# Four buffers instead of three for x and the exponentials, and two moved steps for batches 3 and 4, in a cross-attention and ReGLU kernel

## The chip, the cores and the metric

The kernel runs on one core of a Trainium2 chip. The metric is the device time of one execution in microseconds (us), from the first to the last work of the core; lower is better. Times of runs are medians of several executions. A profile shows one execution, and the times inside it are us from the start of its span.

## The reference

There are 8 batches and 8 heads. Per batch and head, x is 512 rows by 64 and the state is 32 rows by 64. Both attend to each other, and the joined rows go through a gated feed-forward block:

```python
scale = 1.0 / np.sqrt(D)                                  # B, H, S, Ns, D = 8, 8, 512, 32, 64
a  = softmax(scale * x @ state.T)                         # x reads the state
xread = a @ state
a2 = softmax(scale * state @ x.T)                         # the state reads x
sread = a2 @ x
h = concatenate([xread, sread], axis=2)                   # 544 rows a batch, 512 wide after joining heads
gate, val = relu(h @ w_gate), h @ w_val                   # 512 -> 1536
out = (gate * val) @ w_out                                # 1536 -> 512
```

Inputs and output are float32. The kernel computes the matrix products in bfloat16.

## The kernel before, in words

**The work.** The exponentials `e_sn` of the scores serve both softmaxes, since a row sum and a column sum of the same numbers are taken. For a batch b, x comes in as float32 (`xf`), is converted to bfloat16 (`xb`), and is transposed (`xT`). `att_sc` multiplies xT with the transposed state into `sc_ps`, `att_exp` takes the exponential on ScalarE, and `att_norm` sums and divides on VectorE into `a_sn`, which is transposed into `ANS`. The state times the gate and value weights is formed first (`U`), so that the feed-forward input of the 512 x rows is ANS times U. `sr_half` forms the other direction, the state rows, from `e_sn` and `xb`: it is the last reader of both. Eight batches, b = 0 to 7, each have two halves of heads (0 and 1), so `sr_half(0, 1)` is the second half of batch 0.

**Slices.** Each batch is cut in 12 slices jf = 0 to 11 of 128 columns of the 1536. A slice "b.jf" issues, in this order: four matmuls `gv` (L286), `relu` on ScalarE (L311), `mult` on VectorE (L315), and four matmuls of the output product of an earlier slice (`out_piece`, L328). Every third output piece ends a row block: ScalarE copies it (L336) and SyncE's queue (SP) stores it (L337). Behind that, a slice issues the further steps that the table `at(b, jf, step, ...)` names for it, in the order of the calls. The loop is

```python
    for g in range(first, NF * (B + 1)):
        b, jf = divmod(g, NF)
        gv(b, jf) if b < B else gvs(jf)
        relu(b, jf)
        mult(b, jf)
        if g >= lag:
            out_piece(*divmod(g - lag, NF))
        for f in units.get(g, ()):
            f()
```

**What sets the order.** Each engine runs its instructions in the order in which the kernel issues them; no scheduler reorders them. The order in time between engines comes from semaphores that follow the data and from the reuse of buffers: a tile that takes a buffer over waits until the last reader of the tile before it is done. x of batches 1 and 2 is loaded with conversion; x of batch 3 is loaded as float32 by GpSimd (POOL) at the end of its list of loads (`x_dma(3, (nc.gpsimd,))`, L100), and the later ones by SP.

**The steps of the change.** `x_next(b)` is three instructions: two conversions of half a batch on POOL (L147) and one transposing transfer on SP's queue (L154) from `xb` to `xT`. `x_dma(b, (nc.sync,))` is one transfer of 1024 KB on SP's queue (L100) into `xf`, which has two buffers. Slice 2.2 issues `sr_half(0, 0)` and `sr_half(2, 0)`; slice 2.3 issues `sr_half(0, 1)` and then `att_half(3, 0)`, which begins with the score matmuls of batch 3 (L182) that read `xT`; slice 2.4 issues `sr_half(1, 0)` and `sr_half(2, 1)`, slice 2.5 `sr_half(1, 1)` and `att_half(3, 1)`. `xb` and `e_sn` had three buffers each, held by batches 0, 1 and 2 when batch 3 begins; the first of them to be read out is that of batch 0, by `sr_half(0, 1)`.

Of the kernel before, what the change touches and what calls it, by code (L numbers as in the profile page):

```python
# [9 lines left out]
BF16 = mybir.dt.bfloat16  # L10
# [6 lines left out]
def kernel(  # L17
# [9 lines left out]
    nc = tc.nc  # L27

    B, H, S, D = x.shape
    Ns = state.shape[2]  # L30
# [3 lines left out]
    NC = S // 128  # L34
# [3 lines left out]
    def pool(name, bufs, space=None):  # L38
        if space is None:
            return ctx.enter_context(tc.tile_pool(name=name, bufs=bufs))  # L40
        return ctx.enter_context(tc.tile_pool(name=name, bufs=bufs, space=space))
# [4 lines left out]
    att = pool("att", 2)  # L46
# [9 lines left out]
    NK = 2  # L56
    HK = H // NK
# [18 lines left out]
    xf, xb, xT, e_sn, a_sn, ANS, U, hsb, sr_sb = {}, {}, {}, {}, {}, {}, {}, {}, {}  # L76
    copy = {"act": nc.scalar.copy, "dve": nc.vector.tensor_copy, "pool": nc.gpsimd.tensor_copy}

    def bank(name, o=None):

        if o is None:
            return ps_r.tile([128, 512], FP32, name=name, tag="r")
        return ps_o.tile([128, 512], FP32, name=name, tag=f"o{o}")
# [16 lines left out]
            eng.dma_start(out=xf[b][:, i * n:(i + 1) * n], in_=src)  # L100

    def xb_alloc(b):
        xb[b] = att.tile([128, NC * H * D], BF16, name="xb", tag="xb", bufs=3)

    cast_on_load = set()

    def x_dma_cast(b):

        cast_on_load.add(b)
        xb_alloc(b)  # L110
        nc.gpsimd.dma_start(out=xb[b].rearrange("p (h c d) -> p h c d", h=H, c=NC),
                            in_=x[b].rearrange("h (p c) d -> p h c d", c=NC))
        xb[b] = xb[b].rearrange("p (h c d) -> p c h d", h=H, c=NC)
# [28 lines left out]
    def x_conv(b, half, eng):  # L142
        if half == 0:
            xb_alloc(b)
            xb[b] = xb[b].rearrange("p (c h d) -> p c h d", c=NC, h=H)
        hs = slice(HK * half, HK * half + HK)
        copy[eng](out=xb[b][:, :, hs].rearrange("p c h d -> p h c d"), in_=xf[b][:, hs])  # L147
# [25 lines left out]

    def att_sc(b, kc):
        if kc == 0:
            e_sn[b] = att.tile([128, NK, NC, HK * Ns], BF16, name="e_sn", tag="e_sn", bufs=3)
            a_sn[b] = att.tile([128, NK, NC, HK * Ns], BF16, name="a_sn", tag="a_sn")
        t = held["sc", b, kc] = bank("sc_ps")
        ps = t.rearrange("p (c j m) -> p c j m", c=NC, j=2)
        for c in range(NC):  # L180
            for jj in range(2):
                nc.tensor.matmul(ps[:, c, jj], xT[b][:, c, 2 * kc + jj], stT[:, b, 2 * kc + jj],  # L182
                                 start=True, stop=True)
# [218 lines left out]
    def spin(n):  # L402
        for i in range(n):
# [3 lines left out]

    steps = {"spin": spin, "stc": state_conv, "stT": state_T, "sto": state_out, "xc": x_conv, "xT": x_T, "xo": x_out,
             "sc": att_sc, "ex": att_exp, "nm": att_norm, "aT": att_T, "ao": att_out, "aD": att_aT_dma,
             "c": c_unit, "co": c_out, "ga": lambda b, jf: gv(b, jf, (0,)), "gb": lambda b, jf: gv(b, jf, (1,)),  # L410
             "re": relu, "mu": mult, "xn": x_next}
# [23 lines left out]
    def at(b, jf, f, *args):  # L435
        units.setdefault(NF * b + jf, []).append(lambda: f(*args))
# [21 lines left out]
    def att_up(b, kc):  # L458
        att_sc(b, kc)
        att_exp(b, kc)  # L460
        att_norm(b, kc)
# [23 lines left out]
    at(1, 10, att_pe, 2, 1)  # L485
    at(1, 11, u_block, 2, 512)
    at(2, 1, u_block, 2, 1024)
    at(2, 1, x_next, 3)
    at(2, 1, x_dma, 4, (nc.sync,))
    at(2, 2, sr_half, 0, 0)  # L490
    at(2, 3, sr_half, 0, 1)
    at(2, 4, sr_half, 1, 0)
# [19 lines left out]
    for g in range(first, NF * (B + 1)):  # L512
        b, jf = divmod(g, NF)
# [43 lines left out]
```

## Time and profile before

| | |
|---|---|
| median of 3 runs (lowest to highest) | 246.54 us (246.44 to 246.57) |
| the profiled execution: its own time / its span | 245.76 us / 244.0 us |
| busy: TensorE matmul (PE) / VectorE (DVE) / ScalarE (ACT) / GpSimd (POOL) | 226.0 / 145.1 / 123.5 / 27.9 us |
| share of PE in the chain of work that ended last | 83% |
| data moved | 25.72 MB, 105 GB/s in the mean |

How to read it: the page cuts the span in 40 slices of 6.1 us (not the kernel's slices). A digit is the busy share of an engine in tenths, and the row PEclk is the clock that TensorE was granted, in tenths of full speed. In the timeline a row has the start, the duration, the engine, the line and the operation, the tile written and the tiles read, and in square brackets how long the engine was idle before it and what ended that. "SPq" is the queue of SP; its rows are issues of transfers, not the transfers' own time. A matmul of 512 columns has a modelled duration of about 0.38 us, but the next one starts about 0.22 us later, so that the distance between starts is what it costs.

### The profile page before, as it was taken

Reading aid. Unit: us, or ns where it says so; the run is one execution under the profiler, and the core shown is the slowest. Engines: PE = TensorE matmul, PEld = TensorE weight load, DVE = VectorE, ACT = ScalarE, POOL = GpSimd, SP = SyncE. Lnnn points to the kernel's source line nnn. Section 1 sums busy time; section 2 is a strip of 40 time slices with the busy share of each in tenths; the row PEclk is TensorE's granted clock in tenths of the full one; section 3 lists DMA queues with packets and bytes.
Section 4 is the critical chain, followed back from the end, with each engine's and each line's share of the span. In section 5 each row is a group of like instructions: output and inputs, shape, how many; then the busy total and the mean of one; then the engine's idle time right before and its main releaser. Section 6 shows DMA issues by size and latency. Waiting matters only on the chain.

```text
span 244.0 us, 4511 instructions
## 1 busy us (share of the span) xinstructions
PE 226.0 (93%) x1759; PEld 110.6 (45%) x1788; DVE 145.1 (59%) x273; ACT 123.5 (51%) x238; POOL 27.9 (11%) x37
## 2 busy tenths in 40 slices
PE   6698999999089999999999999999999999999994
PEld 2453345345045345534553455345434544666543
DVE  1869785867149666776677667776777634222200
ACT  3768877654013663556355635563556344324221
POOL 8755010000303003000300030000000000000000
PEclk9999999999859999999999999999999999999999
DMA  6999994110471393139313921351141111111142
GB/s 203 183 196 198 223 217 167 46 43 0 79 225 43 80 226 121 46 83 213 142 45 81 259 93 44 84 134 42 46 87 43 46 44 44 46 43 43 64 111 86
DMA packets 36981, 25.72 MB, mean 105 GB/s; under 512 B 17280, under 2 KB 32384, under 8 KB 36960
## 3 DMA queue, kind: packets, MB, share of 16 engines
q1 hardware_dynamic: 25712, 17.31, 25.9%
q0 software_dynamic: 10368, 7.21, 18.5%
q10 hardware_dynamic: 880, 0.92, 1.3%
q8 instruction: 14, 0.23, 0.4%
q14 instruction: 7, 0.06, 0.1%
HBM read 18.35 MB, written 8.91 MB: 112 GB/s over the span
## 4 chain that ended last, share of the span: by engine, by line
PE 83%; DVE 5%; DMA 4%; ACT 2%; issue 2%; POOL 1%; SPq 0%; DVEq 0%; ACTq 0%
PE o_ps L328 35%; PE gv_ps L286 33%; PE gv_ps L304 4%; PE up L261 4%; PE sr_ps L222 3%; DMA xT<-xb 2%; DMA xf<-in_x_dram 2%; PE sc_ps L182 1%; DVE cs L192 1%; DVE a_sn L195 1%; DVE h_sb L315 1%; DMA out_dram<-o_sb 1%; POOL xb L147 1%; PE upc L261 1%; ACT e_sn L186 1%
## 5 line engine op out<-in xcount | busy, mean ns | idle before, releaser
L286 PE MATMUL gv_ps<-ans,U 128*128 128x512 bf16 x359 | 95.9, 382 | 1.5
L328 PE MATMUL o_ps<-wo_sb,h_sb 128*128 128x512 bf16 x370 | 95.8, 382 | 0.3
L311 ACT ACTIVATE g_sb<-gv_ps 128x512 bf16<-128x512 f32 (+1 forms) x108 | 62.5, 579 | 52.2 <-PE gv_ps L286 40.1
L315 DVE TENSOR_TENSOR h_sb<-gv_ps,g_sb 128x512 bf16<-128x512 f32 x96 | 65.5, 690 | 32.4 <-ACT g_sb L311 29.5
L328 PEld LDWEIGHTS <-h_sb 128*128 128x128 bf16 x372 | 36.6, 98 | 42.0 <-issue 1.1
L286 PEld LDWEIGHTS <-U 128*128 128x128 bf16 x384 | 33.7, 98 | 41.9 <-issue 9.6
L336 ACT COPY o_sb<-o_ps 128x512 f32<-128x512 f32 x31 | 18.1, 585 | 22.6 <-PE o_ps L328 22.6
L271 DVE CAST U<-up 128x512 bf16<-128x512 f32 x36 | 23.2, 686 | 6.8 <-PE up L261 6.8
L271 ACT CAST U<-up 128x512 bf16<-128x512 f32 x36 | 19.4, 592 | 11.1 <-PE up L261 11.1
L147 POOL CAST xb<-xf 128x1024 bf16<-128x1024 f32 x10 | 10.1, 1040 | 103.5 <-DMA xf<-in_x_dram 45.9
L192 DVE TENSOR_REDUCE cs<-e_sn 128x16 f32<-128x512 bf16 x16 | 11.0, 685 | 15.3 <-ACT e_sn L186 15.3
L186 ACT ACTIVATE e_sn<-sc_ps 128x512 bf16<-128x512 f32 x16 | 9.6, 600 | 13.0 <-PE sc_ps L182 13.0
L315 DVE TENSOR_TENSOR hs_sb<-gv_ps,g_sb 128x256 bf16<-128x256 f32 x12 | 5.1, 425 | 15.3 <-PE gv_ps L304 10.5
L182 PE MATMUL sc_ps<-stT,xT 128*128 128x64 bf16 x128 | 6.7, 196 | 7.0 <-DMA xT<-xb 6.6
L233 DVE TENSOR_SCALAR sr_sb<-sr_ps,rr 64x128 bf16<-64x128 f32 x32 | 11.2, 350 | 0.8
L195 DVE TENSOR_TENSOR a_sn<-e_sn,rc 128x512 bf16<-128x512 bf16 x16 | 11.1, 692 | 0.6
L222 PE MATMUL sr_ps<-xb,e_sn 128*128 128x256 bf16 x64 | 10.8, 275 | 0.0
L182 PEld LDWEIGHTS <-xT 128*128 128x128 bf16 x128 | 5.7, 100 | 10.4 <-DMA xT<-xb 6.8
L281 ACT CAST U<-upc 128x512 bf16<-128x512 f32 x18 | 9.9, 592 | 0.5 <-PE upc L261 0.5
L261 PEld LDWEIGHTS <-stT 64*32 64x32 bf16 x480 | 4.6, 89 | 11.7 <-issue 11.4
L224 PE MATMUL sr_ps<-ones,e_sn 128*128 128x1 bf16 x64 | 9.2, 166 | 0.0
L261 PE MATMUL up<-wv_sb,stT 64*32 64x512 bf16 x144 | 7.6, 376 | 0.1
(59 smaller groups left out, 138.0 us busy)
## 6 DMA issues: line engine op xcount, KB each, us to landing
out_dram<-o_sb SPq DMA_DIRECT2D x31, 256.0 KB, 2.3
xf<-in_x_dram SPq DMA_DIRECT2D x4, 1024.0 KB, 7.1
wg_sb<-in_moe_w_gate_dram POOLq DMA_DIRECT2D x6, 256.0 KB, 10.3
wv_sb<-in_moe_w_val_dram POOLq DMA_DIRECT2D x6, 256.0 KB, 10.5
wo_sb<-in_moe_w_out_dram POOLq DMA_DIRECT2D x2, 768.0 KB, 15.9
xb<-in_x_dram POOLq DMA_DIRECT2D x2, 512.0 KB, 9.7
xf<-in_x_dram POOLq DMA_DIRECT2D x1, 1024.0 KB, 19.0
xf<-in_x_dram ACTq DMA_DIRECT2D x2, 256.0 KB, 4.3
```

Source lines behind the costliest of these rows:

```text
L147: copy[eng](out=xb[b][:, :, hs].rearrange("p c h d -> p h c d"), in_=xf[b][:, hs])
L182: nc.tensor.matmul(ps[:, c, jj], xT[b][:, c, 2 * kc + jj], stT[:, b, 2 * kc + jj], start=True, stop=True)
L192: nc.vector.reduce_sum(out=cs, in_=e_v, axis=AX.X)
L195: nc.vector.tensor_tensor(out=a_sn[b][:, kc].rearrange("p c (h n) -> p (c h) n", n=Ns), in0=e_v, in1=rc.to_broadcast([128, NC * HK, Ns]), ...
L222: nc.tensor.matmul(ps[:, 0:256], e_sn[b][:, kc, c], xb[b][:, c, HK * kc:HK * kc + HK], start=(c == 0), stop=(c == NC - 1), skip_group_chec ...
L261: nc.tensor.matmul(dst[kc][q:q + 32], stT[r:r + 64, b, j, 32 * sl:32 * sl + 32], wsb[r:r + 64, j, lo:lo + n], start=True, stop=True)
L271: copy[eng](out=U[b][:, w, kc, lo:lo + 512], in_=held["u", b, w, lo][kc])
L286: nc.tensor.matmul(ps[w], U[b][:, w, kc, f0:f0 + 128], ANS[b][:, kc].rearrange("p c t -> p (c t)"), start=(kc == 0), stop=(kc == NK - 1))
L311: nc.scalar.activation(out=g_sb[:, 0:n], in_=ps[0][:, 0:n], func=AF.Relu)
L315: nc.vector.tensor_tensor(out=dst, in0=ps[1][:, 0:n], in1=held["g", b, jf][:, 0:n], op=ALU.mult)
L328: nc.tensor.matmul(o_ps[0], src[:, jf, tsub * 128:(tsub + 1) * 128], wo_sb[:, jf], start=(jf == 0), stop=(jf == NF - 1))
L336: nc.scalar.copy(out=o_sb, in_=o_ps[0])
```

## The change

`xb` and `e_sn` get a fourth buffer. `x_next(3)` is issued at the end of slice 2.0 instead of in slice 2.1, and `x_dma(4)` at the head of what slice 2.4 adds instead of in slice 2.1.

```diff
     def xb_alloc(b):
-        xb[b] = att.tile([128, NC * H * D], BF16, name="xb", tag="xb", bufs=3)
+        xb[b] = att.tile([128, NC * H * D], BF16, name="xb", tag="xb", bufs=4)
...
         if kc == 0:
-            e_sn[b] = att.tile([128, NK, NC, HK * Ns], BF16, name="e_sn", tag="e_sn", bufs=3)
+            e_sn[b] = att.tile([128, NK, NC, HK * Ns], BF16, name="e_sn", tag="e_sn", bufs=4)
...
     at(1, 11, u_block, 2, 512)
     at(2, 1, u_block, 2, 1024)
-    at(2, 1, x_next, 3)
-    at(2, 1, x_dma, 4, (nc.sync,))
+    at(2, 0, x_next, 3)
+    at(2, 4, x_dma, 4, (nc.sync,))
     at(2, 2, sr_half, 0, 0)
```

On POOL the instructions stay in the same order; what they wait for changes. The rows below are the end of POOL's list of loads and the first two pairs of conversions (batch 3, then batch 4); in the brackets are the semaphores waited for: DMASW1 is the load of `xf`, PE the last reader of the buffer that `xb` takes over.

```order
 L100 DMA xf<-in_x_dram 128x8x256 [waits DMASW1_49]
 L125 CAST st_b<-st_f 128x768 [waits DMASW6_49]
-L147 CAST xb<-xf 128x4x4x64 [waits DMASW1_49,DVE_49,PE_49]
+L147 CAST xb<-xf 128x4x4x64 [waits DMASW1_49]
 L147 CAST xb<-xf 128x4x4x64
-L147 CAST xb<-xf 128x4x4x64 [waits DMAHW0_49,DMASW5_49,PE_49]
+L147 CAST xb<-xf 128x4x4x64 [waits DMAHW1_49,DVE_49,PE_49]
 L147 CAST xb<-xf 128x4x4x64
```

The conversion of batch 3 no longer waits for TensorE or VectorE, only for its load; that of batch 4 now takes the buffer of batch 0, which the one of batch 3 took before.

On SP's queue one store changes its place. The rows run from the stores of the first two row blocks (L337), over the transpose of batch 3 (L154) and the load of batch 4 (L100), to the transpose of `a_sn` of batch 3 (L203).

```order
 L337 DMA out_dram<-o_sb 128x512 x2
 L154 DMA_TRANSPOSE xT<-xb 128x16x128
+L337 DMA out_dram<-o_sb 128x512
 L100 DMA xf<-in_x_dram 128x8x256
-L337 DMA out_dram<-o_sb 128x512 x2
+L337 DMA out_dram<-o_sb 128x512
 L203 DMA_TRANSPOSE ans<-a_sn 128x8x128
 L337 DMA out_dram<-o_sb 128x512
```

The store of the third row block (issued by slice 2.2) now stands ahead of the load of batch 4 and not behind it. The lists of PE, DVE and ACT are the same in both kernels.

## The prediction

> **What bounds the kernel now.** I read the head of the page first, then the 40 slices, then the list of waits, and last the timeline where those point.
>
> ```profile
> PE 226.0 (93%) x1759; PEld 110.6 (45%) x1788; DVE 145.1 (59%) x273; ACT 123.5 (51%) x238; POOL 27.9 (11%) x37
> ...
> PE   6698999999089999999999999999999999999994
> ...
> PEclk9999999999859999999999999999999999999999
> ```
>
> TensorE bounds the kernel as a whole, so only what stops or slows it counts. One digit of PE is 0: the eleventh slice, 61.0 to 67.1 us. There and in the slice behind it the granted clock is lower (8, then 5), and nowhere else. The list of waits between 61 and 80 us names the two long ones:
>
> ```profile
> POOL xb L147 <- PE sr_ps L224: 40.1, 2, 30.2
> ...
> PE sc_ps L182 <- DMA xT<-xb: 6.6, 1, 6.6
> ```
>
> The columns are the sum, the number of waits and the longest. The timeline of that place shows how they hang together:
>
> ```profile
> 60.69 0.27 PE L222 MATMUL sr_ps<-xb,e_sn 128*128 128x256 bf16 x1
> ...
> 61.44 2.02 POOL L147 CAST xb<-xf 128x1024 bf16<-128x1024 f32 x2 [30.16 <-PE sr_ps L224]
> ...
> 63.49 1.88 SPq L154 DMA_TRANSPOSE xT<-xb  x1
> 65.55 1.00 SPq L100 DMA_DIRECT2D xf<-in_x_dram  x1
> ...
> 67.97 0.61 PE L182 MATMUL sc_ps<-stT,xT 128*128 128x64 bf16 x8 [6.60 <-DMA xT<-xb]
> ```
>
> POOL stood for 30 us before the conversion of batch 3: the three buffers of xb belonged to batches 0, 1 and 2, and the first comes free when TensorE ends `sr_half(0, 1)` in slice 2.3. But the very next step of TensorE in that slice is the score product of batch 3, which needs conversion, transpose and landing. So the chain of conversion (2.0 us) and transpose (63.49 to 67.97) lies bare in TensorE's path.
>
> **What the pause costs.** Rows of the same steps at full clock, rows of the stretch behind the pause, and the clock there (the column 0.50 of the window):
>
> ```profile
> 56.16 1.04 PE L286 MATMUL gv_ps<-ans,U 128*128 128x512 bf16 x4
> 57.03 1.03 PE L328 MATMUL o_ps<-wo_sb,h_sb 128*128 128x512 bf16 x4
> 57.89 0.27 PE L222 MATMUL sr_ps<-xb,e_sn 128*128 128x256 bf16 x1
> 58.97 1.02 PE L286 MATMUL gv_ps<-ans,U 128*128 128x512 bf16 x3
> ...
> 73.16 0.38 PE L286 MATMUL gv_ps<-ans,U 128*128 128x512 bf16 x1
> ...
> 75.42 0.39 PE L182 MATMUL sc_ps<-stT,xT 128*128 128x64 bf16 x8
> 75.65 0.28 PE L239 MATMUL srT_ps<-id_91,sr_sb 128*128 128x128 bf16 x2
> ```
>
> ```profile
> 68.00:72.20 4.20, 4.20 (x19) 1.92 (x20) 2.32 (x4) 1.19 (x2) 0.00 (x0) 0.50 0.88 286
> ```
>
> Two `sr_half` take 58.97 - 57.89 = 1.08 us, one 0.54. The one that starts at 60.69 therefore leaves TensorE free at 61.23, and the score product starts at 67.97: 6.74 us of pause. Behind it stand scores, four gv, four output matmuls and two sr_half, up to the gv at 73.16: 5.19 us. At full clock these are 0.23 (75.42 to 75.65) + 0.87 (56.16 to 57.03) + 0.86 (57.03 to 57.89) + 1.08 = 3.04 us. The half clock costs 2.15 us more. Together TensorE would gain 8.89 us, if nothing else stopped it.
>
> **Part one: the fourth buffer of xb, and x_next(3) a slice earlier.** The conversion of batch 3 gets a buffer that nobody holds; its wait on TensorE is gone, and it waits only for its load.
>
> ```profile
> 22.40 0.89 POOL L100 DMA_DIRECT2D xf<-in_x_dram  x1 [0.52 <-DMA wg_sb<-in_moe_w_gate_dram]
> ...
> 44.88 7.67 SPq L337 DMA_DIRECT2D out_dram<-o_sb  x2
> ...
> 83.84 0.34 SPq L337 DMA_DIRECT2D out_dram<-o_sb  x1
> 84.28 1.91 SPq L154 DMA_TRANSPOSE xT<-xb  x1
> ```
>
> ```profile
> xf<-in_x_dram POOLq DMA_DIRECT2D x1, 1024.0 KB, 19.0
> ```
>
> ```profile
> DMA to landing us min/median/max: 4.4/4.4/5.6
> ```
>
> The load is issued at 22.4 and lands 19.0 us later, at 41.4 (42.3 if counted from the end of the issue). The two conversions then run to 43.4 or 44.3. On SP's queue the transpose stands behind the stores of two row blocks, the second of which ends its issue at 44.88 + 7.67 = 52.55. The transpose goes out there, right behind a store as at 83.84 and 84.28, and lands 4.4 to 5.6 us later (last fence: the five transposes into xT), at 57.0 to 58.2. TensorE asks at 61.23: 3.0 us to spare. The pause goes wholly, and with it its cause of the half clock. Behind the conversion on POOL stands only that of batch 4; behind the transpose on SP stand the store of slice 2.2 and the load of batch 4, and neither is held longer than now. Issuing x_next(3) in 2.0 instead of 2.1 passes nothing on either queue: 0.
>
> [...] The conversion of batch 3 moves from a quiet place to 41.4 to 44.3, where VectorE is busy with batch 2:
>
> ```profile
> 43.51 0.69 DVE L195 TENSOR_TENSOR a_sn<-e_sn,rc 128x512 bf16<-128x512 bf16 x1
> 44.12 0.42 DVE L171 COPY xT<-xT_ps 128x512 bf16<-128x512 bf16 x1
> ...
> 44.60 0.38 PE L182 MATMUL sc_ps<-stT,xT 128*128 128x64 bf16 x7 [0.33 <-DVE xT L171]
> ...
> 73.36 2.02 POOL L147 CAST xb<-xf 128x1024 bf16<-128x1024 f32 x2 [9.90 <-PE sr_ps L224]
> ...
> 74.73 0.69 DVE L315 TENSOR_TENSOR h_sb<-gv_ps,g_sb 128x512 bf16<-128x512 f32 x1
> ```
>
> A product under a conversion (74.73, inside 73.36 to 75.38) takes the usual 0.69 us, so the near row says 0. But that one reads PSUM and one SBUF tile; the division at 43.51 reads two SBUF tiles, and TensorE waits 0.33 us at 44.60 for the copy behind it, so what it loses TensorE loses. A bound: the division takes double, 0.69 us more; a gain is excluded, since the conversion gives VectorE nothing. I take 0, by the near row. [...]
>
> **Part two: the fourth buffer of e_sn.** The exponential of batch 3 follows the score product, and that follows `sr_half(0, 1)` on TensorE itself, so it finds batch 0's buffer free already: 0 us.
>
> **Part three: the load of batch 4 behind a store.** It stands behind the store whose copy is the first row here; the second row is the size and landing of such loads.
>
> ```profile
> 58.09 0.58 ACT L336 COPY o_sb<-o_ps 128x512 f32<-128x512 f32 x1 [0.47 <-PE o_ps L328]
> ```
>
> ```profile
> xf<-in_x_dram SPq DMA_DIRECT2D x4, 1024.0 KB, 7.1
> ```
>
> The store goes out at about 58.7, the load at about 59.1 (now 65.55), landing near 66.2. Its conversion then ends near 68.3 instead of 75.4 (73.36 + 2.02) and waits for its transpose, which stands behind the store at 83.84 less the gain. It has 7 us to spare. The load begins after xT of batch 3 has landed, so they share nothing: 0.
>
> **What is late next.** The pause also let VectorE catch up. Its rows from the reduction of batch 3 to the product of slice 2.6, and the first work of TensorE that waits for what follows (by the chain of waits):
>
> ```profile
> 61.65 0.71 DVE L233 TENSOR_SCALAR sr_sb<-sr_ps,rr 64x128 bf16<-64x128 f32 x2
> 69.24 0.69 DVE L192 TENSOR_REDUCE cs<-e_sn 128x16 f32<-128x512 bf16 x1 [6.89 <-ACT e_sn L186]
> ...
> 72.83 0.17 DVE L230 RECIPROCAL rr<-sr_ps 128x1 f32<-128x1 f32 x1 [1.16 <-PE sr_ps L224]
> ...
> 75.63 0.17 DVE L230 RECIPROCAL rr<-sr_ps 128x1 f32<-128x1 f32 x1 [0.21 <-PE sr_ps L224]
> ...
> 78.57 0.69 DVE L315 TENSOR_TENSOR h_sb<-gv_ps,g_sb 128x512 bf16<-128x512 f32 x1
> ...
> 80.68 0.23 DVE L245 COPY br<-srT_ps 64x128 bf16<-64x128 bf16 x1 [1.03 <-ACT br L245]
> ```
>
> ```profile
> 80.68 0.24 DVE br L245
> ...
> 80.96 0.40 PE up L261 x4
> ```
>
> From 69.24 to 78.57 VectorE needs 9.33 us with 1.37 us of idling, so 7.96 us without a gap. In the changed kernel the reduction can start at about 62.4: VectorE is done with `sr_norm` at 62.36, and the exponential's result comes no later behind the scores' start than now at half clock (69.24 - 67.97 = 1.27 us, so by 62.5). The product of slice 2.6 then starts at 70.36, 8.2 us earlier. Where nothing waits, a row starts before the last one ends (the row of 43.51 lasts 0.69 us, and the next starts 0.61 us after it); at the two joints where the idling vanishes that saves 0.08 us each: 8.2 to 8.4. I take 8.3. TensorE's `up` at 80.96 hangs on this chain, so from there the kernel is 8.3 us earlier and not 8.89; the difference is a longer wait there, by 0.6 us. VectorE idles 1.03 us in it, so its backlog ends at this place, and all that follows moves as a block.
>
> **Sum.** Against the profiled execution: 245.76 - 8.3 = 237.5 us. The median of the runs is 0.78 us above it: 246.54 - 8.3 = 238.2 us.
>
> **Rivals.**
> - *The division at 43.51 is held by the conversion.* For it: the two lie within 0.1 us or overlap, by when the load lands. Against: 74.73. Time 238.2 + 0.7 = 238.9.
> - *The clock falls all the same.* If the half clock is not the pause's doing, 2.15 us stay, VectorE has its time, and the gain is 6.74: 239.8. Against it: the clock is full in every other slice, where no such pause stands.
> - *The transpose lands late.* If it took twice the longest landing, 11.2 us from 52.55, TensorE would wait from 61.2 to 63.8, and the gain is 8.89 - 2.6 = 6.3: 240.2. Against: the five landings, of which 5.6 is the longest.
> - *It does nothing,* if the early conversion waits for something that I overlook: 246.5. Against: the wait on POOL named the last reader of the buffer, and that is gone.
> - *Slower: an unbroken TensorE is throttled.* From 61.2 us to the end of the span, 244.0 - 8.3 = 235.7, are 174.5 us. If they ran at a granted clock below 0.955, the 8.3 us would be lost (8.3 of 182.8); at 0.94 the time is 249.3. Against it, TensorE works 34.79 of the last 35 us before 240, after 130 us without a pause, at the full clock (the column 1.00):
>
> ```profile
> 205.00:240.00 35.00, 34.79 (x219) 21.53 (x221) 7.17 (x15) 10.54 (x24) 0.00 (x0) 1.00 0.20 69
> ```
>
> **How the numbers follow.** My forecast 0.85; the held division 0.05; the clock 0.03; the late transpose 0.03; nothing 0.02; slower 0.02. A difference under 0.2% (0.5 us) is about what a measurement cannot tell from none. Faster is the first four, 0.96; same 0.02; slower 0.02. The range begins at 237.0, somewhat under 246.54 - 8.89 = 237.7, since TensorE's wait at `up` could shorten where I let it grow, and ends at 239.4, half a us beyond the held division; the other cases, 0.10, are left out.
>
> **What would show it.** Right: no 0 in the PE row and no digit under 9 in PEclk; the conversion of batch 3 at 41 to 44 us behind its load, its transpose issued near 52.6, the load of batch 4 near 59; the score product at about 61.2 with no idle before it; the product of slice 2.6 near 70.3 and a longer wait at the `up` behind it. Wrong: a score product that still waits for xT, a low clock elsewhere, a division of over 0.8 us near 43.5, or a VectorE backlog that reaches beyond slice 2.8.

## The result, and the profile after

| | before | after |
|---|---|---|
| median of 4 runs (lowest to highest) | 246.49 us (245.76 to 246.57) | 238.22 us (237.82 to 240.09) |
| the profiled execution: its own time / its span | 245.76 / 244.0 us | 240.09 / 238.3 us |

The ratio of the times is 0.9687, with a 95% interval of 0.9635 to 0.9740. The forecast was 238.2 us. Two further executions of the changed kernel took 237.59 and 239.83 us. The two rows of the page of the changed kernel, TensorE's busy tenths and its clock in 40 slices of 6.0 us:

```profile
PE   6668999999999999999999999999999999999993
...
PEclk9979999999999999999999999999999999999999
```

The 0 in the PE row is gone, and so is the low clock in the slices where it stood. A 7 in PEclk is new, in the third slice, far ahead of the change; more of that below. The timeline of the changed kernel at the place of the old pause:

```profile
41.84 2.03 POOL L147 CAST xb<-xf 128x1024 bf16<-128x1024 f32 x2 [9.71 <-DMA xf<-in_x_dram]
...
55.41 1.99 SPq L154 DMA_TRANSPOSE xT<-xb  x1
61.43 0.34 SPq L337 DMA_DIRECT2D out_dram<-o_sb  x1
61.94 0.39 SPq L100 DMA_DIRECT2D xf<-in_x_dram  x1
...
63.42 0.27 PE L222 MATMUL sr_ps<-xb,e_sn 128*128 128x256 bf16 x1
...
63.96 0.39 PE L182 MATMUL sc_ps<-stT,xT 128*128 128x64 bf16 x8
```

The conversion now waits for its load alone and runs 20 us earlier; the transpose stands behind the second store; the score product follows `sr_half(0, 1)` after 63.96 - 63.42 = 0.54 us, the length of that step, with no idle time in brackets.

TensorE's rows lie 2.73 us later than forecast (63.42 against 60.69 for the same matmul), and the transpose, the store and the load with them within 0.15 us; only the conversion, which waits for its load alone, does not. The reason is the start of this one execution. These are the rows of the first transposes of x of batch 1 and the gv behind them, before and then after:

```profile
13.01 0.64 PE L165 MATMUL xT_ps<-id_91,xb 128*64 128x128 bf16 x16
13.58 1.90 PE L286 MATMUL gv_ps<-ans,U 128*128 128x512 bf16 x8
```

```profile
14.11 0.94 PE L165 MATMUL xT_ps<-id_91,xb 128*64 128x128 bf16 x16 [1.02 <-DMA xb<-in_x_dram]
14.98 3.22 PE L286 MATMUL gv_ps<-ans,U 128*128 128x512 bf16 x8
```

x of batch 1 landed a us late, and the eight gv took 3.22 us instead of 1.90; the clock was 0.50 from 14.28 to 17.68 us, and 1.00 in the same stretch of the kernel before. Both lie some 27 us ahead of the first step that the change moves, the conversion at 41.84. From there to the old pause the two executions run alike, so the gain is read from the shift: VectorE's product of slice 2.6, forecast at 70.2 to 70.4, against 78.57 before. Below it are the copies of the next step, `state_prep` (it transposes the state of batches 4 to 7), on VectorE and then on ScalarE, and TensorE's products `up`, the second half of which waits for them.

```profile
72.88 0.69 DVE L315 TENSOR_TENSOR h_sb<-gv_ps,g_sb 128x512 bf16<-128x512 f32 x1
73.49 0.47 DVE L139 COPY stT<-stT_ps 64x256 bf16<-64x256 bf16 x2
...
73.93 0.41 PE L261 MATMUL up<-wg_sb,stT 64*32 64x512 bf16 x8
...
74.05 0.63 ACT L139 COPY stT<-stT_ps 64x256 bf16<-64x256 bf16 x2 [3.12 <-DVE stT L139]
...
74.73 0.40 PE L261 MATMUL up<-wv_sb,stT 64*32 64x512 bf16 x4 [0.39 <-ACT stT L139]
75.28 0.40 PE L261 MATMUL up<-wv_sb,stT 64*32 64x512 bf16 x4
75.60 1.04 PE L286 MATMUL gv_ps<-ans,U 128*128 128x512 bf16 x3
```

It is 78.57 - 72.88 = 5.69 us earlier; with the 2.73 us of the start it is 8.42. (245.76 - 240.09 = 5.67 us of the two profiled executions says the same. A later profile of the changed kernel, from the run of it among the experiments, whose start is undisturbed, has this product at 69.69 and the matmul of 60.69 at 60.23: 78.57 - 69.69 - 0.46 = 8.42 us again.) The same rows of the kernel before, for the wait at `up`:

```profile
80.09 0.41 PE L261 MATMUL up<-wg_sb,stT 64*32 64x512 bf16 x8
...
81.29 1.04 PE L286 MATMUL gv_ps<-ans,U 128*128 128x512 bf16 x3
```

### The profile page after: what moved, and what is told of

Same layout as the page of the kernel before. It is cut to its first block, busy times and chain, and to the rows that moved or that the text cites. A ratio compares the mean times of both kernels' runs of the same rounds, so it can differ in the third digit from the quotient of the medians.

```text
span 238.3 us, 4510 instructions
## 1 busy us (share of the span) xinstructions
PE 225.2 (95%) x1759; PEld 110.4 (46%) x1788; DVE 145.0 (61%) x273; ACT 123.4 (52%) x238; POOL 27.9 (12%) x37
## 4 chain that ended last, share of the span: by engine, by line
PE 83%; DVE 5%; DMA 5%; issue 2%; ACT 2%; POOL 2%; POOLq 0%; ACTq 0%
PE o_ps L328 35%; PE gv_ps L286 33%; PE gv_ps L304 4%; PE up L261 4%; DMA xb<-in_x_dram 4%; PE sr_ps L222 3%; DVE h_sb L315 1%; PE sc_ps L182 1%; DVE cs L192 1%; DMA out_dram<-o_sb 1%; PE xT_ps L165 1%; POOL stT L381 1%; PE upc L261 1%; DVE U L281 1%; ACT e_sn L186 0%
## 5 line engine op out<-in xcount | busy, mean ns | idle before, releaser
L261 PEld LDWEIGHTS <-stT 64*32 64x32 bf16 x480 | 4.6, 89 | 12.8 <-issue 12.5
L261 PE MATMUL up<-wg_sb,stT 64*32 64x512 bf16 x144 | 7.4, 386 | 0.0
L222 PEld LDWEIGHTS <-e_sn 128*128 128x128 bf16 x64 | 6.2, 97 | 2.3
```

What stands on the lines that cost most here:

```text
L222: nc.tensor.matmul(ps[:, 0:256], e_sn[b][:, kc, c], xb[b][:, c, HK * kc:HK * kc + HK], start=(c == 0), stop=(c == NC - 1), skip_group_chec ...
L261: nc.tensor.matmul(dst[kc][q:q + 32], stT[r:r + 64, b, j, 32 * sl:32 * sl + 32], wsb[r:r + 64, j, lo:lo + n], start=True, stop=True)
```

## The experiments

Each experiment was timed against the kernel before on the same chip. There were three sessions, each on another chip; the medians of the kernel before were 245.71, 245.72 and 245.74 us, 0.8 below the first chip's, so that ratios and differences are to be compared, not times.

**The buffer alone.** The kernel before with one edit:

```diff
-        xb[b] = att.tile([128, NC * H * D], BF16, name="xb", tag="xb", bufs=3)
+        xb[b] = att.tile([128, NC * H * D], BF16, name="xb", tag="xb", bufs=4)
```

> The kernel before with one edit: xb gets four buffers. x_next(3) and x_dma(4) stay in slice 2.1, e_sn keeps three buffers. Theory (the buffer is the whole gain): the conversion of batch 3 runs at about 41 to 44 us behind its load, its transpose goes out near 52.6 and lands by 58.2, no pause before the score product; 238.2 us as with the full change, within 0.3 us. Rival (the moved steps are needed): the load of batch 4 now follows the transpose at once, at about 54.6, shares the transfer engines with it and delays it past 61.2; then a pause of some us comes back, 239 to 242 us.

Measured: 237.06 us (236.98 to 237.28), 8.65 us below the kernel before; ratio 0.9635 (0.9596 to 0.9674), that of the full change within the intervals. The timeline:

```profile
52.37 2.15 SPq L154 DMA_TRANSPOSE xT<-xb  x1
54.72 0.85 SPq L100 DMA_DIRECT2D xf<-in_x_dram  x1
...
60.92 0.39 PE L182 MATMUL sc_ps<-stT,xT 128*128 128x64 bf16 x8
```

The load of batch 4 follows the transpose at once, and the score product has no idle time before it. The transpose has enough to spare, so the rival falls. (The five transposes into xT landed 4.4 to 5.7 us after their issue in this run.)

**All but the buffer.** The changed kernel with `bufs=3` for xb.

> The changed kernel with xb back at three buffers: four buffers for e_sn and both moved steps stay. Theory: the conversion of batch 3 waits for sr_half(0, 1) as before, the score product for its transpose; 246.5 us, within 0.3 us of the kernel before. Rival (issuing x_next a slice earlier is worth something by itself): 238 to 245 us.

Measured: 245.85 us; ratio 1.0013 (0.9977 to 1.0049). The list of waits has the old pause:

```profile
PE sc_ps L182 <- DMA xT<-xb: 6.5, 1, 6.5
```

So without the buffer of xb, the moved steps and the fourth buffer of e_sn are worth nothing that can be measured. With it that rests on two chips: 8.65 us for the buffer alone here, 8.27 us for the full change in the result, and the intervals of the two ratios overlap.

**The pause kept, TensorE kept busy in it.** The kernel before, and in slice 2.3

```diff
     at(2, 3, sr_half, 0, 1)
+    at(2, 3, fill, 28)          # 28 matmuls of the warm-up's zeros into a spare bank
```

> The kernel before with 28 matmuls of no use (128x512, the zeros of the warm-up, into a bank that nobody reads) between sr_half(0, 1) and the score product of batch 3, about 6.05 us of TensorE work inside its pause of 6.74. The pause stays. Theory (the half clock is the pause's doing): the clock stays full behind it; TensorE's steps there shrink by 2.15 us, but VectorE's chain of 7.96 us from the reduction (now at about 69.0) allows 1.6 to 1.7: 244.8 to 244.9 us. Rival (the half clock has another cause): 246.5 us, or more by the work added.

Measured: 243.73 us (243.65 to 244.06), 1.98 us below; ratio 0.9908 (0.9873 to 0.9943). The filling, the score product, VectorE's product of slice 2.6, and the window behind the pause (columns: length, busy time of the engines, and third from the end the clock):

```profile
61.21 6.20 PE L470 MATMUL fill_ps<-warm 128*128 128x512 bf16 x28
...
67.92 0.41 PE L182 MATMUL sc_ps<-stT,xT 128*128 128x64 bf16 x8 [0.50 <-DMA xT<-xb]
...
76.75 0.69 DVE L315 TENSOR_TENSOR h_sb<-gv_ps,g_sb 128x512 bf16<-128x512 f32 x1
```

```profile
68.00:72.20 4.20, 4.20 (x38) 2.50 (x39) 3.06 (x7) 1.68 (x3) 0.00 (x0) 1.00 0.86 288
```

The score product starts as late as before (67.97), but the clock is 1.00 where it was 0.50. So the half clock behind this pause is the doing of TensorE's idleness in it. The gain at 76.75 is 1.82 us and not TensorE's 2.15, because VectorE's chain sets it; I had 1.6 to 1.7. The 1.98 us of the medians are more than that, and the 8 executions lie within 0.41 us of one another, where the 19 of the kernel before on the same chip spread over 3.1 us.

**VectorE's backlog taken away.** The changed kernel with two steps of slice 2.6 moved behind the products of slice 2.7 (`sr_fin` transposes what `sr_half` formed, and copies it):

```diff
-    at(2, 6, state_prep, 4, B)
-    at(2, 6, sr_fin, 0)
+    at(2, 10, state_prep, 4, B)
+    at(2, 10, sr_fin, 0)
```

> The changed kernel with state_prep(4, B) and sr_fin(0) moved from slice 2.6 to slice 2.10. Theory (VectorE's backlog from slices 2.3 to 2.6 makes TensorE wait at the products up of slice 2.7, since their banks are still held by the two steps that VectorE and ScalarE copy late): that wait, 1.1 us in the trace of the changed kernel, goes, and the time is 237.1 to 237.3 us. Rival (the backlog only shows in another place): 238.2 us.

Measured: 235.95 us (235.87 to 237.61); ratio 0.9599 (0.9556 to 0.9643). On the same chip the kernel with the buffer alone took 237.06, so this one takes 1.11 us less. The products of slice 2.7 and the gv behind them:

```profile
71.72 0.41 PE L261 MATMUL up<-wg_sb,stT 64*32 64x512 bf16 x8
71.95 0.40 PE L261 MATMUL up<-wv_sb,stT 64*32 64x512 bf16 x8
72.28 1.10 PE L286 MATMUL gv_ps<-ans,U 128*128 128x512 bf16 x4
```

From the first `up` to the gv it is 0.56 us now. In the changed kernel it was 75.60 - 73.93 = 1.67, in the kernel before 81.29 - 80.09 = 1.20: the change made this wait longer by 0.47 us. The kernel with the buffer alone has 72.57 - 70.89 = 1.68 there, so the wait is the whole 1.11. It is the shortest version on that chip.

**The changed kernel again.** On the chip of the next three.

> The changed kernel once more, on the chip of the next three, to hold them against it and to see how its executions spread. Theory (the spread comes from the first 20 us, where TensorE waits for loads and in some executions loses the full clock for a while, in both kernels alike): executions in two groups about 2 us apart, and 8.3 to 8.7 us below the kernel before in the medians. Rival (the change itself makes the start slower at times): the kernel before shows one group only.

Measured: 237.46 us (236.91 to 239.01) against 245.72 (244.69 to 246.69); ratio 0.9684 (0.9651 to 0.9718). The difference is 8.26 us, at the edge of the 8.3 to 8.7 expected. The executions do spread over 2.1 us, but the 11 of the kernel before over 2.0, and neither shows two clean groups on this chip: 236.91, 236.92, 237.00, then 237.91, 238.57, 239.01. On the first session's chip the kernel before does show two: 13 executions up to 245.98 us and 6 from 247.18 us on. This run doesn't say whether the start makes them.

**The conversion made twice, to cover VectorE's division.** The changed kernel, in x_next(3), with both halves of the conversion issued a second time.

> The changed kernel with the two conversions of batch 3 on POOL made twice, the second time over the same result, so that POOL works for 4.05 us from about 41.5 and covers VectorE's division of batch 2 (two SBUF inputs, 0.69 us when alone). Nothing else waits for the second pair but the transpose, which goes out behind the store at 52.6 anyway. Theory (VectorE is not held): the division stays at 0.69 us and the time is that of the changed kernel within 0.3 us. Rival (GpSimd and VectorE contend there): a division of 0.8 to 1.4 us and a time longer by as much, since TensorE waits for the copy behind it.

Measured: 238.16 us (237.91 to 238.90), 0.7 above the changed kernel in the medians; ratio 0.9701 (0.9673 to 0.9728). The changed kernel's own executions spread over 2.1 us on this chip, so that the times alone don't decide, and the traces have to. The conversions, the division and the score product of batch 2, first of this kernel, then of the changed kernel on the same chip:

```profile
41.00 2.02 POOL L147 CAST xb<-xf 128x1024 bf16<-128x1024 f32 x2 [9.52 <-DMA xf<-in_x_dram]
42.97 2.48 POOL L398 CAST xb<-xf 128x1024 bf16<-128x1024 f32 x2
...
43.23 1.32 DVE L195 TENSOR_TENSOR a_sn<-e_sn,rc 128x512 bf16<-128x512 bf16 x1
...
44.94 0.38 PE L182 MATMUL sc_ps<-stT,xT 128*128 128x64 bf16 x7 [0.96 <-DVE xT L171]
```

```profile
41.18 2.02 POOL L147 CAST xb<-xf 128x1024 bf16<-128x1024 f32 x2 [9.81 <-DMA xf<-in_x_dram]
...
43.04 0.70 DVE L195 TENSOR_TENSOR a_sn<-e_sn,rc 128x512 bf16<-128x512 bf16 x1
...
44.13 0.38 PE L182 MATMUL sc_ps<-stT,xT 128*128 128x64 bf16 x7 [0.34 <-DVE xT L171]
```

Under a conversion the division took 1.32 us instead of 0.70, the pair of conversions 2.48 instead of 2.02, and TensorE waited 0.62 us longer (0.96 against 0.34). My theory falls and the rival holds: beside each other both took longer. GpSimd lost 0.46 us, and 0.62 us is the price of this one placement, seen in one execution. In the changed kernel the conversion ends at 43.20 and the division starts at 43.04, so they touch for 0.16 us only, and the division took 0.70 us; it was the time of the load's landing that spared it.

**Three buffers, the first read out earlier.** The kernel before with

```diff
+    at(1, 10, sr_half, 0, 0)
+    at(1, 10, sr_half, 0, 1)
...
-    at(2, 2, sr_half, 0, 0)
-    at(2, 3, sr_half, 0, 1)
```

> The kernel before, with its three buffers and its steps x_next(3) and x_dma(4) in slice 2.1, but with sr_half(0, 0) and sr_half(0, 1) moved from slices 2.2 and 2.3 to slice 1.10. Theory (what matters is when the first buffer comes free, not how many there are): batch 0's buffer is free near 51.5, the conversion runs to 53.6, the transpose lands by 58.2, and the pause is gone; 8.3 to 9 us below the kernel before, as with the fourth buffer. Rival (the fourth buffer is needed, since the steps moved make VectorE late in slices 1.10 and 1.11 instead): a gain of 4 to 8 us.

Measured: 237.43 us (236.85 to 238.54), 8.29 us below the kernel before; ratio 0.9672 (0.9644 to 0.9700), the same as the changed kernel's on that chip.

```profile
51.54 2.02 POOL L147 CAST xb<-xf 128x1024 bf16<-128x1024 f32 x2 [19.95 <-PE sr_ps L224]
...
54.35 2.17 SPq L154 DMA_TRANSPOSE xT<-xb  x1
...
61.83 0.40 PE L182 MATMUL sc_ps<-stT,xT 128*128 128x64 bf16 x8
```

The conversion still waits for TensorE, but 10 us earlier, and the score product finds its transpose. What counted was when a buffer comes free.

**Both edits that help, and TensorE kept busy in the start.** The kernel with state_prep and sr_fin in slice 2.10, and

```diff
-    c.1.0 c.0.0 spin.2 aT.0.0 spin.1 aT.0.1 ...
+    c.1.0 c.0.0 spin.4 aT.0.0 spin.5 aT.0.1 ...
```

which puts warm-up matmuls in gaps near 10 and 12 us: two more ahead of the first transposes of a_sn of batch 0 and four more between those and the second.

> The changed kernel with state_prep(4, B) and sr_fin(0) in slice 2.10 (as in the run with that one edit), and with two more warm-up matmuls ahead of the first transposes of a_sn of batch 0 and four more behind them, in gaps of 0.6 and 1.0 us where TensorE waits for VectorE. Theory (the slow executions lose the clock in the first 14 us because TensorE stands too often there): one group of executions, about 9.7 us below the kernel before, without those 2 us longer. Rival (the clock there does not hang on such gaps, or the loads are late anyway): two groups as before, or all executions longer by up to 0.5 us.

Measured: 236.00 us (235.88 to 236.07, 5 executions), 9.72 us below the kernel before and within 0.2 us of one another; ratio 0.9607 (0.9586 to 0.9629). The median is that of the edit without the matmuls (235.95 on another chip). An execution like the 237.61 there, one of six, is not among these five; that the matmuls are the reason is likely but not shown by so few.

**The same matmuls in the changed kernel, and in the kernel before.**

> The changed kernel with the two and four more warm-up matmuls in the first 13 us, and nothing else. Theory (TensorE's standing there costs the full clock in some executions, of either kernel): no execution with half clock, all within 0.5 us of each other, at the level of the short executions of the changed kernel, 236.9 to 237.9 by the chip. Rival (the tight group of the run with both edits was luck): some executions 1.5 to 2.5 us longer, as without the matmuls.

> The kernel before with the same six matmuls. Theory: its longer executions (1.5 to 2.5 us over its shortest) go, and the difference to the changed kernel with these matmuls is the cleanest measure of the change: 8.3 to 8.5 us. Rival (the start is not what spreads the executions): the same spread as the kernel before.

Measured: 237.28 us (236.94 to 237.38, 6 executions) for the changed kernel, 245.91 (245.15 to 246.35, 12 executions) for the one before, whose unedited executions in that session reached 247.82, three of 17 above 247. With the matmuls the changed kernel varies by 0.44 us. The kernel before shows none of its longest executions, but its 11 executions in the second session, without the matmuls, had none above 247 either, and a spread of 1.2 us stays: the forecast that the start alone spreads it was wrong. The record points at the pause instead. In the first session 10 of 31 executions of the two kernels with an idle pause (the one before, and all but the buffer) lay above 247 us; of the 20 of the other three only one, the 237.61, lay more than 0.5 us above the shortest of its kernel. Part of the spread is likely the half clock behind the pause, which lasted 6.8 us in one trace and 10.2 us in another. In the trace of the kernel before with the matmuls:

```profile
62.00:63.00 1.00, 0.00 (x0) 0.00 (x0) 0.00 (x0) 0.00 (x0) 1.00 (x2) 0.95 0.00 0
63.00:64.00 1.00, 0.00 (x0) 0.00 (x0) 0.00 (x0) 0.00 (x0) 0.00 (x1) 0.50 0.00 0
...
73.00:74.00 1.00, 1.00 (x8) 0.58 (x7) 0.92 (x4) 0.15 (x1) 0.58 (x1) 0.93 0.00 0
```

and in that of the kernel before:

```profile
65.00:66.00 1.00, 0.00 (x0) 0.00 (x0) 0.00 (x0) 0.00 (x0) 0.00 (x0) 0.80 1.16 214
...
72.00:73.00 1.00, 1.00 (x13) 0.85 (x12) 0.17 (x1) 0.00 (x0) 0.00 (x0) 0.78 0.03 12
```

In the kernel before the clock goes from 1.00 to 0.50 within 0.1 us (65.6 to 65.7), so I read a us at 0.95 as 0.9 us at full clock and 0.1 at half. By this the clock was halved from 62.9 to 73.1 us in the one, from 65.6 to 72.4 in the other, although the pauses began at the same place within 0.5 us (60.91 and 61.37, the ends of the last matmul ahead of them). The difference of the medians with the matmuls, 8.63 us, lies above the 8.3 to 8.5 expected, and it holds a cost of the half clock that varies.

## Why the prediction was right, point by point

- **The pause, 6.74 us:** right. It is gone in the changed kernel and with the buffer alone, and whole without it (6.5 us of waiting).
- **The half clock, 2.15 us:** right as the pause's doing, shown by filling the pause with work (a clock of 1.00 from 68.0 to 72.2 us instead of 0.50). The amount is one execution's: the half clock behind the score product lasts from 67.97 to 72.4 in the profile of before, from 67.52 to 73.1 in another.
- **The landing of the load, the place of the transpose behind the second store, the load of batch 4 near 59:** right (conversion at 41.18, transpose at 52.22 and load at 58.76 in the later, undisturbed profile of the changed kernel; 41.84, 55.41 and 61.94 in the first).
- **The fourth buffer of e_sn and the two moved steps, 0:** right within what the two halves of the change can show: 1.0013 (0.9977 to 1.0049) without the buffer of xb, overlapping intervals with it.
- **VectorE's chain, which takes the gain from 8.89 to 8.2 to 8.4:** right at 8.42. In the rows, `up` waits for ScalarE's copy of `state_prep`, that for VectorE's copy, and that stands behind the product of slice 2.6. The cause is shown: with the two steps of slice 2.6 out of its way the time falls by 1.11 us. The changed kernel's wait there grew by 0.47 us; I had 0.6.
- **The division at 43.51, taken at 0 from the product at 74.73:** the number held, the reason did not. The near row was the wrong one: that product, with one input in PSUM, took 0.69 us under a conversion, and a division, with two in SBUF, took 1.32 us under one, against 0.70 in the changed kernel. That the place of the inputs makes the difference no run shows by itself. The bound, a division that takes double, was an estimate of mine; the run with the second conversion came near it, and the rival's price of 0.7 us is near what it cost there (0.62 us of waiting). In the changed kernel the step was saved by luck in the landing: the conversion ended 0.16 us behind the division's start in one profile, 0.18 ahead of it in another (42.90 and 43.08, the kernel with both edits and the matmuls), and a landing later by 0.7 us would have put most of the division under it.
- **What I missed:** the start. The profile of before showed one execution, in which TensorE kept its clock there (1.00 from 13 to 18 us); two profiles, of the changed kernel and of the one with state_prep late, lose it for 3.4 us (14.28 to 17.68 and 12.8 to 16.2, at 0.50). No profile of the kernel before shows that. It moved the profiled execution of the changed kernel by 2.73 us, out of the range, though not the median, and it is the low clock elsewhere that my list names as a sign of being wrong; the pause's place shows none.
- **What was luck:** that the median meets the forecast within 0.02 us. The changed kernel, the buffer alone and the early read-out lay 8.26 to 8.65 us below the kernel before in the later sessions, so that the last tenths are chance. The sum also carries over the 0.78 us by which the median of before lies above its profiled execution, and no run shows what they are made of: the kernel before has a half clock that varies, the changed one a start that varies.

## What to carry to other kernels

A wait of TensorE for a transfer is followed back until something free of data stands there: here a buffer, whose last reader stood directly ahead of its next user. Freeing it earlier did the same here as adding one (8.29 us against 8.26). And the pause gave VectorE time to catch up, so its price, 8.89 us, was not what came back, 8.42: add up the busiest engine's work behind it before the gain is written down, and look at what that engine holds.

## What the runs showed of the hardware that I had not expected

The clock was lost here without a long gap as well. Windows of 3.4 us, as long as the shortest stretch of half clock in these traces, up to the moment where it was halved, with TensorE's busy time as the second figure: the kernel before with the added matmuls (halved from 62.9 us), the changed kernel's start (from 14.3 us), and the start of the kernel with state_prep late (halved from 12.8 us, third from the end 0.88 in its row of 12 to 13 us). Last, a window of the kernel before at the pause's beginning, behind which the clock stayed full:

```profile
59.50:62.90 3.40, 1.42 (x13) 0.76 (x10) 2.09 (x6) 0.24 (x1) 1.92 (x2) 1.00 0.00 0
```

```profile
10.88:14.28 3.40, 1.39 (x16) 0.77 (x18) 2.45 (x6) 1.84 (x4) 0.44 (x1) 1.00 1.42 191
```

```profile
9.30:12.70 3.40, 1.76 (x29) 0.64 (x13) 3.11 (x7) 2.18 (x5) 2.00 (x3) 1.00 1.41 187
```

```profile
58.80:62.20 3.40, 2.52 (x21) 1.38 (x18) 2.98 (x10) 0.60 (x1) 0.76 (x1) 1.00 0.00 0
```

In the second and third of these no gap was over 1.1 us long, yet TensorE was busy for only 41% and 52% of the window; in the first, busy for 42%, the gap had lasted 2.0 us when the clock fell; behind the last, at 74%, the clock stayed at 1.00 until 65.6 us, 4.2 us into the pause. The stretches of half clock lasted 3.4 us in the two starts (14.28 to 17.68 and 12.8 to 16.2) and 6.8 us (65.6 to 72.4) and 10.2 us (62.9 to 73.1) in and behind the two pauses, twice and three times as long. What sets these lengths, no run shows. Nor does any show that the busy share is what counted: three windows suggest it, no run was made for it alone, and no limit comes out of them. The changed kernel's window from 4.04 to 7.45 us holds 1.77 us of work, 52% as well, and the clock stayed at 1.00 behind it, up to 14.2 us.
